# A linear-attention and routed-MLP block: how tile 3 is transposed, where the inverse deviation of the first tiles is computed, and two loads moved

## The chip, the cores and the metric

The kernel runs on one core of one Trainium2 chip. The metric is the device time of one launch in microseconds. The core's engines each run their own instruction queue in order: TensorE (PE, with its weight loads shown apart as PEld), VectorE (DVE), ScalarE (ACT), GpSimd (POOL) and SyncE (SP), which here only issues DMAs. Semaphores order them against each other.

## What is computed

x has 2048 rows (tokens) of 640 columns, in bf16. The result is the sum of three parts:

```python
xn  = layernorm(x)                       # (x - mean) / sqrt(var + 1e-5), per row
q, k, v = split(xn @ wqkv)               # 32 heads of 20 columns
phi(t) = where(t > 0, t + 1, exp(t)) + 1e-6
kv  = phi(k)^T v   per head              # sums over all 2048 rows
z   = sum over rows of phi(k)
A   = (phi(q) kv) / (phi(q) z) @ wo
r   = xn @ w_r;  the 8 rows with the largest r
y   = (silu(xn_sel @ w_gate) * (xn_sel @ w_up)) @ w_down * sigmoid(r_sel)
out = x + A + xn + (y added on the 8 chosen rows)
```

## The kernel before

The 2048 rows are 16 tiles of 128 rows; the 640 columns are 5 chunks of 128. The order of the instructions on every engine is the order in which the program writes them; the framework only adds the semaphore waits.

**Front part, tile by tile (t = 0 to 15).** For each tile:

- `ln_a`, `ln_b`, `ln_g` (VectorE): statistics of the left and the right half of the row, then mean and variance.
- `ln_r` (ScalarE): the inverse deviation `SR`, by a logarithm and an exponential.
- `ln_xn` (VectorE): the normalized tile, written to `XX[:, t, 0, :]`.
- The transposed tile `xnT`: tiles 0 to 3 by TensorE into PSUM (`tr_mm`, five 128x128 transposes in two halves) and from there by a copy on ScalarE or VectorE (`tr_cp`); tiles 4 to 15 by a DMA transpose issued on SP (`tr_dma`).
- `K` (TensorE): the tile's k, in two halves of 320 columns (the second half has one more, r), five matmuls each. For tiles 0 to 3 each half is cut again into chunks 0 and 1 (`KA`) and chunks 2 to 4 (`KB`), which are written between other work. The weights of the two halves, `wkh[0]` and `wkh[1]`, are loaded apart, the first on ScalarE's queue, the second on SP's.
- `PHe`, `PHr` (ScalarE) and `PHb` (VectorE): exponential, relu and their combination `pk`, that is phi(k).
- `G` (TensorE): sums of xn times phi(k) over the rows, accumulated in PSUM over all tiles, five matmuls of 512 columns and four of 128 for each tile. `ones(t)` (GpSimd) overwrites one column of the normalized tile with 1 after its transpose has been taken, so that `G` gives z too.

The first four tiles are written out by hand, interleaved; from tile 4 on a loop does `K(t)`, then `PHb(t-1)`, the normalization of tile t+2 with its DMA transpose, the phi of tile t, the statistics of tile t+3, and `G(t-1)`. Some turns of the loop also build constants on GpSimd (`pool_extra`).

**x on SP's queue.** Tiles 0 to 3 are loaded one by one, then the second half of the k weights, then tiles 4 to 7, 8 to 11 and 12 to 15 in three loads, then a DMA transpose of a block of zeros.

**After the front part.** The queries (`q_pe`, `q_fin`) follow in 20 steps, with the choice of the 8 rows, the gate and up products, the denominators and the folded output matrix between them, and at the end the output tiles. `bm2`, a mask made on GpSimd by `consts_e` and `bm2_copies`, is first used between the queries and the output.

The scratch tile for the phi of k and the PSUM banks matter for the order: `K` of tiles 0, 2 and 3 uses banks 6 and 7, that of tile 1 banks 4 and 5, the transposes of tiles 0 and 2 banks 0 and 1, those of tiles 1 and 3 banks 2 and 3, and `G` banks 0 to 5.

Of the kernel before, what the change touches and what calls it, by code (L numbers as in the profile page):

```python
# [7 lines left out]
P = 128  # L8
S = 2048
D = 640  # L10
# [3 lines left out]
T = S // P  # L14
KC = D // P
# [8 lines left out]
EPS_BF16 = 1.0013580322265625e-05  # L24
# [6 lines left out]
F32 = mybir.dt.float32  # L31
# [3 lines left out]
ALU = mybir.AluOpType  # L35
# [3 lines left out]
def kernel(  # L39
# [13 lines left out]
    pe, dve, act, pool, sp = nc.tensor, nc.vector, nc.scalar, nc.gpsimd, nc.sync  # L53

    x_v = A_x[0].rearrange("(t p) d -> p t d", p=P)
    out_v = out[0].rearrange("(t p) d -> p t d", p=P)
    wqkv_v = A_wqkv.rearrange("(kc p) n -> p kc n", p=P)
# [9 lines left out]
    def st(shape, dt, name, tag=None):  # L67
        return sb.tile(shape, dt, name=name, tag=tag or name)

    XX = st([P, T, 2, D], BF16, "XX")  # L70
# [10 lines left out]
    wu = st([P, KC, F], BF16, "wu")  # L81
# [5 lines left out]
    lowkey = st([P, T], I32, "lowkey")  # L87
    eps6 = st([P, 1], F32, "eps6")
    eps5 = st([P, 1], F32, "eps5")
    lnv = st([P, T], F32, "lnv")  # L90
    rbf = st([P, T], BF16, "rbf")
    MVf = st([P, T, 2], F32, "MVf")
    MV = MVf[:].bitcast(BF16).rearrange("p t (k o) -> p t k o", o=2)[:, :, :, 1]
    SR = st([P, T], F32, "SR")
# [3 lines left out]
    HW = 320  # L98
    wkh = [wk[:, :, 0:HW], wk[:, :, HW + 64 :]]


    def ld(eng, dst, src):
        eng.dma_start(dst, src)
# [7 lines left out]
    ld(act, wkh[0], wqkv_v[:, :, D : D + HW])  # L111
    ld(sp, XX[:, 1, 1, :], x_v[:, 1, :])
    ld(sp, XX[:, 2, 1, :], x_v[:, 2, :])
    ld(sp, XX[:, 3, 1, :], x_v[:, 3, :])
    ld(sp, wkh[1][:, :, 0:HW], wqkv_v[:, :, D + HW : 2 * D])
    for a, b in ((4, 8), (8, 12), (12, 16)):
        ld(sp, XX[:, a:b, 1, :], x_v[:, a:b, :])
    sp.dma_start_transpose(xnT[:, 0:4, S - P : S], zero[:])

    def warm4(w):  # L120
        pe.matmul(PS[:, 7, 0:w], lhsT=nc.const_aps.tensor(0.0, (P, P), F32),
                  rhs=nc.const_aps.tensor(0.0, (P, w), F32), start=True, stop=True)

    dve.memset(eps5[:], EPS_BF16)
    pool.memset(ident[:], 0.0)
    pool.affine_select(
        out=ident[:], in_=ident[:], compare_op=ALU.not_equal, fill=1.0,
# [19 lines left out]
    def ln_a(t):  # L147
        sts[t] = tmp.tile([P, 2, nc.vector.BN_STATS_DIM], F32, tag="stats", name="stats", bufs=4)
        dve.bn_stats(out=sts[t][:, 0, :], in_=XX[:, t, 1, 0:320])  # L149

    def ln_b(t):
        dve.bn_stats(out=sts[t][:, 1, :], in_=XX[:, t, 1, 320:D])  # L152

    def ln_g(t):
        dve.bn_aggr(out=MV[:, t, :], in_=sts[t][:])

    def ln_r(t):
        act.activation(lnv[:, t : t + 1], MV[:, t, 1:2], AF.Ln, bias=eps5[:])
        act.activation(SR[:, t : t + 1], lnv[:, t : t + 1], AF.Exp, scale=-0.5)  # L159

    def ln_xn(t, parts=((0, D),)):
        for a, b in parts:
            dve.tensor_scalar(out=XX[:, t, 0, a:b], in0=XX[:, t, 1, a:b], scalar1=MVf[:, t, 0:1],  # L163
                              scalar2=SR[:, t : t + 1], op0=ALU.subtract, op1=ALU.mult)
# [3 lines left out]
    def tr_mm(t, h, b0):  # L168
        k0, k1 = TRP[h]
        pt = PS[:, b0 + h, :].bitcast(BF16)  # L170
        for kc in range(k0, k1):
            pe.transpose(pt[:, (kc - k0) * P : (kc - k0 + 1) * P], XX[:, t, 0, kc * P : (kc + 1) * P], ident[:])  # L172

    def tr_cp(t, h, b0, eng):
        k0, k1 = TRP[h]
        src = PS[:, b0 + h, :].bitcast(BF16)[:, 0 : (k1 - k0) * P].rearrange("p (k c) -> p k c", c=P)
        dst = xnT[:, k0:k1, t * P : (t + 1) * P]
        if eng is act:
            act.copy(dst, src)  # L179
        else:  # L180
            dve.tensor_copy(dst, src)

    def tr_dma(t):
        sp.dma_start_transpose(xnT[:, :, t * P : (t + 1) * P], XX[:, t, 0, :])
# [14 lines left out]
    def off(t, h):  # L199
        return T - 1 - t if t != 1 and h else 0  # L200

    def K(t, hs=(0, 1), b=6, ks=range(KC)):
        for h in hs:
            if t > 4:
                pad(1)
            w = HW + h
            for kc in ks:
                pe.matmul(  # L208
                    PS[:, b + h, off(t, h) : off(t, h) + w],
                    lhsT=xnT[:, kc, t * P : (t + 1) * P],  # L210
                    rhs=wkh[h][:, kc, 0:w],
                    start=(kc == 0),
                    stop=(kc == KC - 1),
                )
# [3 lines left out]
    def phi_src(t, h, b):  # L218
        return PS[:, b + h, off(t, h) : off(t, h) + HW]

    def PHe(t, h, b=6):
        if t not in phis:
            phis[t] = tuple(tmp.tile([P, D], BF16, tag=k, name=k, bufs=3) for k in ("ek", "rk"))
        act.activation(phis[t][0][:, h * HW : (h + 1) * HW], phi_src(t, h, b), AF.Exp)  # L224

    def PHr(t, h, b=6):
        act.activation(phis[t][1][:, h * HW : (h + 1) * HW], phi_src(t, h, b), AF.Relu)  # L227
# [13 lines left out]
    def PHb(t):  # L241
        ek, rk = phis[t]
        dve.scalar_tensor_tensor(out=pk[:, t, :], in0=ek[:], scalar=1.0, in1=rk[:], op0=ALU.min, op1=ALU.add)  # L243

    def pad(n):
        for _ in range(n):
            pe.ldweights(zero[:, 0:P])  # L247

    def G(t, ks=range(KC)):
        for a in ks:  # L250
            lhsT = XX[:, t, 0, a * P : (a + 1) * P]
            pe.matmul(  # L252
                PS[:, a, :], lhsT=lhsT, rhs=pk[:, t, 0:512],
                start=(t == 0), stop=(t == T - 1),
            )
            if t > 4:
                pad(2)
            if a < 4:
                pe.matmul(  # L259
                    PS[:, 5, a * P : (a + 1) * P], lhsT=lhsT, rhs=pk[:, t, 512:D],  # L260
                    start=(t == 0 and a == 0), stop=(t == T - 1), skip_group_check=True,
                )

    def ones(t):
        pool.memset(XX[:, t, 0, ZD : ZD + 1], 1.0)  # L265
# [12 lines left out]
    def band(ap, base, n, w=DH):  # L278
        for k, (b0, sg) in enumerate(((base, 1), (w - 1 - base, -1))):
            pool.affine_select(  # L280
                out=ap, in_=ap, compare_op=ALU.is_ge, fill=0.0,
                base=b0, pattern=[[-sg * w, n], [0, w]], channel_multiplier=sg,
            )

    def consts_e():
        pool.memset(bm2[0:E2, :], 1.0)
        band(bm2[0:E2, :], P, 8)

    def bm2_copies(gs):
        for g in gs:  # L290
            pool.tensor_copy(bm2[32 * g : 32 * g + 32, :], bm2[0:E2, :])
# [14 lines left out]
    def consts_d():  # L306
        pool.iota(lowkey[:], pattern=[[P, T]], base=P - 1, channel_multiplier=-1)

    pool_extra = {3: consts_b, 4: consts_c, 5: consts_d}

    wo_v = A_wo.rearrange("(g r) d -> r g d", r=GC)
    wg_v = B_w_gate.rearrange("(kc p) n -> p kc n", p=P)
    wu_v = B_w_up.rearrange("(kc p) n -> p kc n", p=P)
# [18 lines left out]
                ld(sp, wg[:, k, :], wg_v[:, k, :])  # L332


    consts_e()
    bm2_copies((1, 2, 3))
    KA, KB = (range(0, 2), range(2, KC))
    ln_a(0)
    ln_b(0)
    ln_a(1)  # L340
    ln_g(0)
    ln_b(1)
    ln_r(0)
    ln_g(1)
    ln_xn(0, ((0, 2 * P),))
    ln_r(1)
    ln_xn(0, ((2 * P, D),))
    tr_mm(0, 0, 0)
    ln_xn(1)
# [5 lines left out]
    tr_cp(0, 1, 0, act)  # L355
    K(0, (0,), 6, KA)
    ln_b(2)
    tr_cp(1, 0, 2, act)
    tr_mm(1, 1, 2)
    ones(1)  # L360
    K(0, (0,), 6, KB)
    tr_cp(1, 1, 2, act)
    ln_g(2)
    ln_a(3)
    K(1, (0,), 4, KA)
    ln_r(2)
    ln_b(3)
    K(1, (0,), 4, KB)
    PHe(0, 0, 6)
    ln_xn(2)  # L370
    K(0, (1,), 6, KA)
    PHr(0, 0, 6)
    K(1, (1,), 4, KA)
    ln_g(3)
    ln_r(3)
    tr_mm(2, 0, 0)
    K(0, (1,), 6, KB)
    tr_cp(2, 0, 0, act)
    tr_mm(2, 1, 0)
    ones(2)  # L380
    ln_xn(3)
    K(1, (1,), 4, KB)
    PHe(0, 1, 6)
    tr_cp(2, 1, 0, dve)
    PHr(0, 1, 6)
    tr_mm(3, 0, 2)
    ln_a(4)
    K(2, (0,), 6, KA)
    rcopy1(5)
    PHe(1, 0, 4)  # L390
    tr_mm(3, 1, 2)
    ones(3)
    PHb(0)
    K(2, (1,), 6, KA)
    PHr(1, 0, 4)
# [4 lines left out]
    PHr(1, 1, 4)  # L400
    PHe(2, 0, 6)
    G(0, (4,))
    tr_cp(3, 0, 2, dve)
    ln_g(4)
    G(0, (0,))
    PHr(2, 0, 6)
    tr_cp(3, 1, 2, dve)
    G(0, (1,))
    ln_r(4)
    PHb(1)  # L410
    G(0, (2,))
    K(3, (0,), 6, KA)
    PHe(2, 1, 6)
    G(0, (3,))
    ln_xn(4)
    PHr(2, 1, 6)
    K(3, (0,), 6, KB)
    ln_a(5)
    tr_dma(4)
    ones(4)  # L420
    K(3, (1,), 6, KA)
    ln_b(5)
    PHe(3, 0, 6)
    G(1)
    PHr(3, 0, 6)
    ln_g(5)
    PHb(2)
    ln_r(5)
    ln_xn(5)
    K(3, (1,), 6, KB)  # L430
    tr_dma(5)
    ones(5)
    G(2)
    PHe(3, 1, 6)
    PHr(3, 1, 6)
    ln_a(6)
    ln_b(6)
    ln_g(6)
# [53 lines left out]
    for t in range(T - 1):  # L492
# [13 lines left out]
                      op0=ALU.arith_shift_right, op1=ALU.bitwise_and)  # L506
# [21 lines left out]
    def z_ev():  # L528
        dve.tensor_copy(zs[:, 0:512], PS[0:1, 4, :])
        dve.tensor_copy(zs[:, 512:D], PS[0:1, 6, 0:P])  # L530
        ld(sp, zcol[:], zs[:])
# [275 lines left out]
    q_fin(0, 0)  # L807
    q_pe(0, 1, 7)
    z_ev()
    for k0, k1 in ((0, 3), (3, KC)):  # L810
        ld(sp, wu[:, k0:k1, :], wu_v[:, k0:k1, :])
    q_pe(0, 2, 1)
    q_fin(0, 1)
    q_pe(0, 3, 2)
# [137 lines left out]
```

## Time and profile before

| | |
|---|---|
| median of 3 runs | 105.94 us (105.9 to 106.11) |
| the profiled execution | 105.91 us |
| its span (first to last instruction) | 104.2 us |
| TensorE busy | 99.8 us (96% of the span) |
| VectorE busy | 82.7 us (79%) |
| ScalarE busy | 69.1 us (66%) |
| GpSimd busy | 17.1 us (16%) |
| TensorE's granted clock | full in all 40 slices |
| bytes moved by DMA | 19.77 MB, 190 GB/s on average |

Times in the profile are microseconds from the start of the span. A row of a timeline has start, duration, engine, line of the kernel, operation, what it writes and reads with the shape, how many are merged in the row, and in brackets how long the engine was idle before it and what ended the wait. A row of a group has, after the bar, the busy time and the mean duration in ns. A row of DMA issues has the bytes of one and the microseconds from issue to landing. "PE" with line 208 is `K`, 172 `tr_mm`, 252 and 259 `G`; "DVE" with line 149, 152 and 155 is `ln_a`, `ln_b` and `ln_g`, 163 `ln_xn`, 181 `tr_cp`, 243 `PHb`; "ACT" with 158 and 159 is `ln_r`.

### The profile page before, as it was taken

To read this page: it belongs to the slowest core of one execution; us is meant where nothing else is said; L and a number is where in the kernel's file an instruction comes from. 1 tells how busy PE (TensorE), PEld (TensorE's weight loads), DVE (VectorE), ACT (ScalarE), POOL (GpSimd) and SP (SyncE) were. 2 spreads that over 40 slices of the span, in tenths; PEclk is the share of its full clock that TensorE was granted. 3 is DMA by queue.
4 is the path that set the end of the run, shared out by engine and by line. 5 is a ranking of instruction groups with operands and counts; after the bars stand their busy time and mean duration, and the time that the engine had idled before them with its cause. 6 is when DMAs were issued, how large, how long until landed. Compare 5 with 4: busy or idle time off the path is not lost.

```text
span 104.2 us, 2816 instructions
## 1 busy us (share of the span) xinstructions
PE 99.8 (96%) x944; PEld 72.5 (70%) x1176; DVE 82.7 (79%) x186; ACT 69.1 (66%) x174; POOL 17.1 (16%) x57
## 2 busy tenths in 40 slices
PE   6999999999999999999999999999999999999980
PEld 3347666668888888888877777875577667777760
DVE  1797999988888898873887886778988997888870
ACT  4289957666666666888599989997983997000000
POOL 7700000620000000000000064460001500000500
PEclk9999999999999999999999999999999999999999
DMA  2999937334557755889999999901760039983344
GB/s 63 298 307 377 325 66 69 66 66 92 135 127 92 140 124 124 191 248 359 224 399 249 360 406 382 319 22 31 217 236 9 12 110 270 280 289 122 126 129 126
DMA packets 23408, 19.77 MB, mean 190 GB/s; under 512 B 10978, under 2 KB 21858, under 8 KB 23394
## 3 DMA queue, kind: packets, MB, share of 16 engines
q1 hardware_dynamic: 22152, 19.11, 63.2%
q10 hardware_dynamic: 954, 0.46, 1.7%
q8 instruction: 8, 0.13, 0.6%
q0 software_dynamic: 288, 0.01, 0.3%
q14 instruction: 6, 0.05, 0.2%
HBM read 13.80 MB, written 3.65 MB: 168 GB/s over the span
## 4 chain that ended last, share of the span: by engine, by line
PE 89%; DVE 3%; DMA 2%; issue 2%; DVEq 0%
PE PS L208 21%; PE PS L480 21%; PE PS L751 20%; PE PS L252 16%; PE PS L259 4%; DMA XX<-in_A_x_dram 2%; PE PS L708 2%; PE PS L672 1%; PE PS L551 1%; PE PS L172 1%; PE PS L727 1%; PE PS L273 1%; DVE stats L149 1%; DVE XX L163 1%; DVE stats L152 1%
## 5 line engine op out<-in xcount | busy, mean ns | idle before, releaser
L208 PE MATMUL PS<-wk,xnT 128*128 128x320 bf16 (+1 forms) x160 | 25.2, 300 | 0.0
L252 PE MATMUL PS<-pk,XX 128*128 128x512 bf16 x75 | 22.7, 379 | 0.0
L247 PEld LDWEIGHTS <-zero 128*128 128x128 bf16 x224 | 18.2, 97 | 5.7
L480 PE MATMUL PS<-xnT,wq 128*128 128x512 bf16 x97 | 21.8, 379 | 0.3 <-issue 0.2
L751 PE MATMUL PS<-Mb,pqT 128*128 128x320 bf16 (+4 forms) x165 | 22.1, 295 | 0.0
L224 ACT ACTIVATE ek<-PS 128x320 bf16<-128x320 f32 x32 | 14.1, 441 | 9.9 <-PE PS L208 9.9
L751 PEld LDWEIGHTS <-pqT 128*128 128x128 bf16 x165 | 15.8, 98 | 4.5 <-issue 0.2
L208 PEld LDWEIGHTS <-xnT 128*128 128x128 bf16 x160 | 15.1, 97 | 4.5 <-ACT xnT L179 0.2
L243 DVE SCALAR_TENSOR_TENSOR pk<-ek,rk 128x640 bf16<-128x640 bf16 x16 | 13.1, 820 | 4.8 <-ACT rk L227 4.5
L542 DVE SCALAR_TENSOR_TENSOR pqT<-qe,qr 128x512 bf16<-128x512 bf16 x20 | 13.5, 682 | 2.5 <-ACT qr L489 2.5
L488 ACT ACTIVATE qe<-PS 128x512 bf16<-128x512 f32 x20 | 12.5, 624 | 2.9 <-PE PS L480 2.3
L259 PE MATMUL PS<-pk,XX 128*128 128x128 bf16 x64 | 14.0, 219 | 0.3
L227 ACT ACTIVATE rk<-PS 128x320 bf16<-128x320 f32 x32 | 14.0, 437 | 0.0
L480 PEld LDWEIGHTS <-wq 128*128 128x128 bf16 x100 | 11.6, 118 | 2.9
L489 ACT ACTIVATE qr<-PS 128x512 bf16<-128x512 f32 x20 | 12.5, 626 | 0.0
L760 DVE TENSOR_TENSOR o<-PS,XX 128x640 bf16<-128x640 f32 x11 | 9.0, 823 | 2.9 <-PE PS L751 1.4
L252 PEld LDWEIGHTS <-XX 128*128 128x128 bf16 x80 | 7.8, 98 | 4.5
L196 ACT ACTIVATE XX<-XX,MR,SR 128x640 bf16<-128x640 bf16 x11 | 9.4, 913 | 0.0
L149 DVE BATCH_NORM_STATS2 stats<-XX 128x6 f32<-128x320 bf16 x16 | 7.4, 461 | 2.0 <-DMA XX<-in_A_x_dram 2.0
L163 DVE TENSOR_SCALAR XX<-XX,MVf,SR 128x640 bf16<-128x640 bf16 (+2 forms) x17 | 7.2, 433 | 0.6 <-ACT SR L159 0.6
L152 DVE BATCH_NORM_STATS2 stats<-XX 128x6 f32<-128x320 bf16 x16 | 7.7, 482 | 0.0
L265 POOL MEMSET XX<- 128x1 bf16 x18 | 1.9, 107 | 35.4 <-DVE XX L163 15.5
(111 smaller groups left out, 102.1 us busy)
## 6 DMA issues: line engine op xcount, KB each, us to landing
out_dram<-o SPq DMA_DIRECT2D x15, 160.0 KB, 2.7
XX<-in_A_x_dram SPq DMA_DIRECT2D x3, 640.0 KB, 7.9
wg<-in_B_w_gate_dram SPq DMA_DIRECT2D x5, 384.0 KB, 7.7
wd<-in_B_w_down_dram SPq DMA_DIRECT2D x1, 1920.0 KB, 13.3
wu<-in_B_w_up_dram SPq DMA_DIRECT2D x1, 1152.0 KB, 6.3
wv<-in_A_wqkv_dram SPq DMA_DIRECT2D x5, 160.0 KB, 2.6
wq<-in_A_wqkv_dram SPq DMA_DIRECT2D x1, 800.0 KB
hi_d<-XX SPq DMA_DIRECT2D x1, 800.0 KB, 4.0
```

What stands on the lines that cost most here:

```text
L208: pe.matmul(PS[:, b + h, off(t, h) : off(t, h) + w], lhsT=xnT[:, kc, t * P : (t + 1) * P], rhs=wkh[h][:, kc, 0:w], start=(kc == 0), stop=( ...
L224: act.activation(phis[t][0][:, h * HW : (h + 1) * HW], phi_src(t, h, b), AF.Exp)
L227: act.activation(phis[t][1][:, h * HW : (h + 1) * HW], phi_src(t, h, b), AF.Relu)
L243: dve.scalar_tensor_tensor(out=pk[:, t, :], in0=ek[:], scalar=1.0, in1=rk[:], op0=ALU.min, op1=ALU.add)
L247: pe.ldweights(zero[:, 0:P])
L252: pe.matmul(PS[:, a, :], lhsT=lhsT, rhs=pk[:, t, 0:512], start=(t == 0), stop=(t == T - 1),)
L259: pe.matmul(PS[:, 5, a * P : (a + 1) * P], lhsT=lhsT, rhs=pk[:, t, 512:D], start=(t == 0 and a == 0), stop=(t == T - 1), skip_group_check= ...
L480: pe.matmul(PS[:, bank, :], lhsT=by5(wq[:, kc, :])[:, m, :], rhs=xnT[:, kc, tb * TBLK : (tb + 1) * TBLK], start=(kc == 0), stop=(kc == KC ...
L488: act.activation(e, PS[:, bank, :], AF.Exp)
L489: act.activation(r, PS[:, bank, :], AF.Relu)
L542: dve.scalar_tensor_tensor(out=pqT[:, m, tb * TBLK : (tb + 1) * TBLK], in0=e, scalar=1.0, in1=r, op0=ALU.min, op1=ALU.add,)
L751: pe.matmul(PS[:, b, o : o + c1 - c0], lhsT=pqT[:, kc, t * P : (t + 1) * P], rhs=Mb[:, kc, c0:c1], start=(kc == 0), stop=(kc == KC - 1))
```

## The change

- Tile 3 is transposed by a DMA on SP instead of five transposes on TensorE and two copies on VectorE. Its `K` is no longer spread over the sums of tiles 0 and 1 but stands behind `G(1)`, in whole halves; `PHe(3, ...)`, `PHr(3, ...)` and the instructions around it move with it.
- The inverse deviation of tiles 0 to 3 is computed on GpSimd, by an add of the epsilon and a power of -0.5 (`ln_p`), instead of two instructions on ScalarE. A constant column of -0.5 is set by VectorE at the start.
- On VectorE the first part of `ln_xn(0)` stands ahead of `ln_g(1)`; `ln_a(3)` and `ln_b(3)` stand behind `ln_xn(2)`.
- On SP the second half of the k weights is loaded ahead of x of tile 3. The load of x of tiles 12 to 15 moves behind the DMA transpose of tile 3.
- The mask `bm2` is made in the loop's turn for tile 7 instead of at the start; the two loads of the up weights become one.

```diff
+    mhalf = st([P, 1], F32, "mhalf")
...
     ld(sp, XX[:, 1, 1, :], x_v[:, 1, :])
     ld(sp, XX[:, 2, 1, :], x_v[:, 2, :])
+    ld(sp, wkh[1][:, :, 0:HW], wqkv_v[:, :, D + HW : 2 * D])
     ld(sp, XX[:, 3, 1, :], x_v[:, 3, :])
-    ld(sp, wkh[1][:, :, 0:HW], wqkv_v[:, :, D + HW : 2 * D])
-    for a, b in ((4, 8), (8, 12), (12, 16)):
+    for a, b in ((4, 8), (8, 12)):
         ld(sp, XX[:, a:b, 1, :], x_v[:, a:b, :])
     sp.dma_start_transpose(xnT[:, 0:4, S - P : S], zero[:])
...
+    dve.memset(mhalf[:], -0.5)
...
+    def ln_p(t):
+        pool.tensor_scalar(out=lnv[:, t : t + 1], in0=MV[:, t, 1:2], scalar1=EPS_BF16, scalar2=None, op0=ALU.add)
+        pool.tensor_tensor(out=SR[:, t : t + 1], in0=lnv[:, t : t + 1], in1=mhalf[:], op=ALU.pow)
...
+    def consts_f():
+        consts_e()
+        bm2_copies((1, 2, 3))
-    pool_extra = {3: consts_b, 4: consts_c, 5: consts_d}
+    pool_extra = {3: consts_b, 4: consts_c, 5: consts_d, 6: consts_f}
...
-    consts_e()
-    bm2_copies((1, 2, 3))
     KA, KB = (range(0, 2), range(2, KC))
     ln_a(0)
     ln_b(0)
     ln_a(1)
     ln_g(0)
+    ln_p(0)
     ln_b(1)
-    ln_r(0)
+    ln_xn(0, ((0, 2 * P),))
     ln_g(1)
-    ln_xn(0, ((0, 2 * P),))
-    ln_r(1)
+    ln_p(1)
     ln_xn(0, ((2 * P, D),))
     tr_mm(0, 0, 0)
     ln_xn(1)
...
     ln_b(2)
+    ln_g(2)
+    ln_p(2)
...
     tr_cp(1, 1, 2, act)
-    ln_g(2)
-    ln_a(3)
     K(1, (0,), 4, KA)
-    ln_r(2)
-    ln_b(3)
     K(1, (0,), 4, KB)
     PHe(0, 0, 6)
     ln_xn(2)
+    ln_a(3)
+    ln_b(3)
     K(0, (1,), 6, KA)
     PHr(0, 0, 6)
     K(1, (1,), 4, KA)
     ln_g(3)
-    ln_r(3)
+    ln_p(3)
     tr_mm(2, 0, 0)
     K(0, (1,), 6, KB)
     tr_cp(2, 0, 0, act)
     tr_mm(2, 1, 0)
     ones(2)
     ln_xn(3)
+    tr_dma(3)
+    ones(3)
+    ld(sp, XX[:, 12:T, 1, :], x_v[:, 12:T, :])
     K(1, (1,), 4, KB)
     PHe(0, 1, 6)
     tr_cp(2, 1, 0, dve)
     PHr(0, 1, 6)
-    tr_mm(3, 0, 2)
     ln_a(4)
...
-    tr_mm(3, 1, 2)
-    ones(3)
     PHb(0)
...
     G(0, (4,))
-    tr_cp(3, 0, 2, dve)
     ln_g(4)
     G(0, (0,))
     PHr(2, 0, 6)
-    tr_cp(3, 1, 2, dve)
     G(0, (1,))
     ln_r(4)
     PHb(1)
     G(0, (2,))
-    K(3, (0,), 6, KA)
     PHe(2, 1, 6)
     G(0, (3,))
     ln_xn(4)
     PHr(2, 1, 6)
-    K(3, (0,), 6, KB)
     ln_a(5)
     tr_dma(4)
     ones(4)
-    K(3, (1,), 6, KA)
+    G(1)
     ln_b(5)
-    PHe(3, 0, 6)
-    G(1)
-    PHr(3, 0, 6)
     ln_g(5)
+    K(3, (0,), 6)
     PHb(2)
     ln_r(5)
+    PHe(3, 0, 6)
     ln_xn(5)
-    K(3, (1,), 6, KB)
+    K(3, (1,), 6)
+    PHr(3, 0, 6)
     tr_dma(5)
     ones(5)
-    G(2)
     PHe(3, 1, 6)
     PHr(3, 1, 6)
+    G(2)
...
-    for k0, k1 in ((0, 3), (3, KC)):
-        ld(sp, wu[:, k0:k1, :], wu_v[:, k0:k1, :])
+    ld(sp, wu[:], wu_v)
```

## The prediction

> **What bounds the kernel now.** The page first: how long the span is, which engine is full, and what the chain of waits is made of.
>
> ```profile
> span 104.2 us, 2816 instructions
> PE   6999999999999999999999999999999999999980
> PE 89%; DVE 3%; DMA 2%; issue 2%; DVEq 0%
> ```
>
> TensorE is full in every slice but the first and the last, and 89% of the chain is its own instructions. So the time is a start, then a block of matmuls without a gap, then a short end. Only two things can move it: matmul work taken out of the block, and a gap put in front of it or into it. The profiled execution took 105.91 us, 1.71 more than its span; the median of the runs is 105.94, so the sum below is made against 105.91 and carries over as it is.
>
> The chain in order of time shows where the block begins, and where the change touches it.
>
> ```profile
> 5.54 0.80 DVE XX L163 x2
> 6.38 0.29 PE PS L172 x2
> ...
> 9.90 0.13 PE PS L172 x2
> 10.03 0.27 PE PS L208 x2
> 10.30 0.17 PE PS L172 x3
> 10.47 1.09 PE PS L208 x8
> 11.56 0.22 PE PS L252
> ```
>
> Up to 6.3 us the normalization of tiles 0 and 1 on VectorE is the chain; from 6.38, the first transposes of tile 1, it is TensorE alone. The five L172 pieces at 9.90 and 10.30 are the transposes of tile 3. At 11.56 the sums G(0) begin (the record of their first matmul starts at 11.40, since a record begins before the array streams). Next, the engine that feeds this stretch: VectorE's timeline (start, duration).
>
> ```profile
> 4.48 0.20 DVE L155 BATCH_NORM_AGGREGATE MVf<-stats 128x2 bf16<-128x12 f32 x1
> ...
> 5.27 1.05 DVE L163 TENSOR_SCALAR XX<-XX,MVf,SR 128x256 bf16<-128x256 bf16 x3
> 6.23 0.49 DVE L149 BATCH_NORM_STATS2 stats<-XX 128x6 f32<-128x320 bf16 x1
> 6.64 0.48 DVE L152 BATCH_NORM_STATS2 stats<-XX 128x6 f32<-128x320 bf16 x1
> 7.15 0.21 DVE L155 BATCH_NORM_AGGREGATE MVf<-stats 128x2 bf16<-128x12 f32 x1
> 7.27 0.44 DVE L149 BATCH_NORM_STATS2 stats<-XX 128x6 f32<-128x320 bf16 x1
> 7.63 0.48 DVE L152 BATCH_NORM_STATS2 stats<-XX 128x6 f32<-128x320 bf16 x1
> 8.08 0.45 DVE L163 TENSOR_SCALAR XX<-XX,MVf,SR 128x640 bf16<-128x640 bf16 x1
> 8.44 0.20 DVE L155 BATCH_NORM_AGGREGATE MVf<-stats 128x2 bf16<-128x12 f32 x1
> 9.24 0.45 DVE L163 TENSOR_SCALAR XX<-XX,MVf,SR 128x640 bf16<-128x640 bf16 x1 [0.60 <-ACT SR L159]
> 9.61 0.35 DVE L181 COPY xnT<-PS 128x384 bf16<-128x384 bf16 x1
> 9.87 0.49 DVE L149 BATCH_NORM_STATS2 stats<-XX 128x6 f32<-128x320 bf16 x1
> 10.27 0.81 DVE L243 SCALAR_TENSOR_TENSOR pk<-ek,rk 128x640 bf16<-128x640 bf16 x1
> ...
> 19.03 0.83 DVE L243 SCALAR_TENSOR_TENSOR pk<-ek,rk 128x640 bf16<-128x640 bf16 x1
> 19.77 0.44 DVE L163 TENSOR_SCALAR XX<-XX,MVf,SR 128x640 bf16<-128x640 bf16 x1
> ```
>
> The three L163 of the 5.27 row end at 6.32; the last, ln_xn(1), is one of 0.45, so it began at 5.87. The row at 10.27 is PHb(0), which ends at 11.08; G(0) reads its pk. (The two rows at 19 us serve a question below.) So G(0) had 0.32 us to spare, and a VectorE that comes to PHb(0) later than that stops TensorE. This is the place that decides.
>
> **The price of the moved deviation.** Now it is two ScalarE instructions, of which the first stands here, with the first matmul of G(0).
>
> ```profile
> 4.71 0.29 ACT L158 ACTIVATE lnv<-MVf,eps 128x1 f32<-128x1 bf16 x1 [0.63 <-DVE MVf L155]
> 11.40 0.38 PE L252 MATMUL PS<-pk,XX 128*128 128x512 bf16 x1
> ```
>
> From the end of the aggregate (4.68) to the L163 that uses the result (5.27) are 0.59 us, with a hop of 0.03 at its start (4.68 to 4.71), and I take the same at its end. The new path is hop, add on GpSimd, its wait for its own result, power, hop; call it p. No row shows a power on GpSimd. The nearest:
>
> ```profile
> L265 POOL MEMSET XX<- 128x1 bf16 x18 | 1.9, 107 | 35.4 <-DVE XX L163 15.5 <-DMA xnT<-XX 12.9 <-DVE MVf L155 3.2
> L291 POOL COPY bm<-bm 32x160 bf16<-32x160 bf16 x3 | 0.9, 310 | 0.1
> L651 POOL COPY kv<-kv 32x40 bf16<-32x40 bf16 x4 | 0.8, 210 | 1.3 <-DVE kv L640 1.2
> 18.88 0.12 POOL L295 MEMSET bm<- 128x32 f32 x1
> 19.08 0.85 POOL L297 TENSOR_SCALAR_AFFINE_SELECT bm<-bm 128x32 f32<-128x32 f32 x1
> L297 POOL TENSOR_SCALAR_AFFINE_SELECT bm<-bm x2: 288/568/849, 19.1 to 20.0; 128x32 f32<-128x32 f32 x2
> ```
>
> The copies give 0.10 us for 120 columns more, so one column costs 0.18; the memset at 18.88 ends at 19.00 and the select that needs it starts at 19.08, a wait of 0.08. I take 0.18 for the add and, for want of a nearer row, as much for the power: p = 0.03 + 0.18 + 0.08 + 0.18 + 0.03 = 0.50. Lower end: both as cheap as a memset, 0.10, p = 0.34. Upper end: the add like the quicker of the selects of L297 (0.29), the power like their mean (0.57), p = 1.00. The path itself is thus worth about what ScalarE's is; what counts is how often VectorE now stands and waits for it.
>
> **The change step by step, at p = 0.50.**
>
> Tile 0 and 1: ln_xn(0)'s first part now comes before ln_g(1). Power of tile 0 at 4.68 + 0.50 = 5.18; first part to ln_g(1) 0.27 (5.27 to the 5.54 of the chain), ln_g(1) 0.21 (as at 7.15), end 5.66. Its power ends at 6.16, where ln_xn(1) starts, 0.29 later than now. ln_xn(0)'s rest (0.36) lies inside that wait. The two deviations, side by side before, are in series now.
>
> Tile 2: ln_a(2) follows 0.36 on, ln_b(2) 0.41, ln_g(2) 0.51, its end 0.21 (rows from 5.87 to 7.36: 1.49). Before, ln_a(3) and ln_b(3) filled the wait for the deviation; the change moves them behind ln_xn(2), so VectorE idles for p: ln_xn(2) at 6.16 + 1.49 + 0.50 = 8.15, against 8.08.
>
> Tile 3: ln_a(3) 0.36 later, at 8.51, then the same 0.41, 0.51 and 0.21 to the end of ln_g(3) at 9.64, and p again: ln_xn(3) at 10.14, against 9.24. That is 0.90 later.
>
> From there the order is unchanged: copy of tile 2, ln_a(4), PHb(0), which ends 1.84 after ln_xn(3) starts (9.24 to 11.08): 11.98. TensorE's first matmul starts some 0.08 behind it (ln_xn(1) ends at 6.32, its transposes stand at 6.38), at 12.06. Before it was 11.40. Hence **+0.66 us**.
>
> What TensorE saves in front of that: the five transposes, 0.13 + 0.17 = 0.30. Without a stall G(0) would come 0.30 earlier; with it the 0.30 only lengthens the stall, so I count it at nothing. It would count in full if PHb(0) ended by 11.0.
>
> The second weight half and x of tile 3 swap on SP's queue.
>
> ```profile
> 2.68 0.43 SPq L103 DMA_DIRECT2D wk<-in_A_wqkv_dram  x1
> wk<-in_A_wqkv_dram SPq DMA_DIRECT2D x1, 400.0 KB, 5.4
> xnT<-XX SPq DMA_TRANSPOSE x12, 3.2
> xnT<-zero SPq DMA_TRANSPOSE x1, 8.0
> ```
>
> The later of the two lands at 2.68 + 5.4 = 8.1 now, with the same bytes ahead of it after the swap; so x of tile 3 lands near 8.1, under the 8.51 at which ln_a(3) wants it: nothing at p = 0.50. At p = 0.34 ln_a(3) could go at 8.03 and waits for it, 0.1.
>
> Tile 3's transpose by DMA: issued at the end of ln_xn(3), 10.6, landing 3.2 later, 13.8. K(3) is behind G(0) and G(1), ten matmuls of 0.22 after 12.06 at the least, so not before 14.2: covered by 0.4. The zero transpose took 8.0 because it stood behind all x loads; the load of tiles 12 to 15 (640 KB) no longer stands in front. That load waits on SP behind tile 3's transpose, and tile 4's transpose behind both; its cover is K(3) and G(2). x of tile 12 is first read in turn 8 of the loop. ones(3) waits for the transpose on GpSimd, with only other ones behind it, and the last power is ahead. Two copies of tile 3 leave VectorE behind PHb(0), 0.6 us that G(1)'s PHb(1) can use: no gap of its own between G(0) and G(1). ScalarE loses eight small instructions; it is not what PHb(0) waits for then. The mask constants moved to turn 7 (about 2 us of GpSimd, used only after the queries) and the joined load of wu (one issue less on SP, weights wanted late) are counted at nothing; cover: GpSimd's idle time of 2.5 us a turn, and the whole query stage.
>
> Sum: 105.91 + 0.66 = 106.57, said as 106.6. In p it is four waits in a row (ln_xn(3) at 8.14 + 4p), so 0.1 more in p is 0.4 in the time. The ends: p = 0.34 with x at 8.1 gives ln_xn(3) at 9.6, G(0) at 11.5, 106.0; p = 1.00 gives ln_xn(3) 12.14, G(0) 14.06, 108.6.
>
> **A rule weighed.** The row first: the two selects of L297 are the same instruction, one took 0.85 us, the other 0.29; the first began at 19.08 with the pass of 19.03 to 19.86 running, the second at 20.0 with the L163 of 19.77 to 20.21. The Trainium skill, GPSIMD Engine Reference, section 8 (Key points), says that GpSimd shares its SBUF interfaces with VectorE and contends with VectorE instructions in a two-port mode or with two SBUF inputs; by that the first select was held, and the trace agrees; the second, beside a one-input pass, does not show it. By that rule the sum would be 106.8, without it 106.6; the working is the first rival.
>
> **Rivals.**
> *GpSimd is held by VectorE.* Tile 1's add comes at 5.69, while ln_xn(0)'s rest (0.36, from about 5.57) still runs; if it is held until 5.93, ln_xn(1) and all behind it are 0.24 later: 106.8. For it: the 0.85 of L297. Against: the 0.29 of the second. Part of the slower cases, 0.12. The page of the Trainium skill named above speaks for this one.
> *The transposes' gain comes through: faster.* G(0) stands the whole 0.30 earlier if ln_xn(3) starts by 9.16, which needs p = 0.26 (8.14 + 4p) and x of tile 3 by 7.8: 105.6. It turns faster at all below ln_xn(3) = 9.48, p = 0.33. For it: the durations on GpSimd are rough, and its waits may overlap; one of ScalarE's deviations now takes 0.72 (aggregate end 7.36 to 8.08), since ScalarE is crowded. Against: both of GpSimd's instructions would have to be cheaper than a memset, and x of tile 3 now arrives last. 0.13.
> *It cancels.* p of 0.33 to 0.38, G(0) within 0.2 of 11.40: 105.9 to 106.1. 0.14.
> *Late transposes or a slow power.* If tile 3's or 4's transpose lands like the zero one did, or the power costs a microsecond, TensorE stops again: tile 3 landing at 10.6 + 8.0 = 18.6, where K(3) is due at 14.2 or later, would cost up to 4.4 more, 111; a power of 1 us, p = 1.3, gives ln_xn(3) at 13.3 and 109.8. Against: the queue has 640 KB less in front. 0.07.
>
> **How the numbers follow.** The forecast (VectorE reaches PHb(0) late, +0.2 to +1.6) has 0.54, its held form 0.12, together with the last rival 0.73 for slower by over 0.2%, about what a measurement of this kernel can tell from no change (0.21 us); same 0.14, faster 0.13. The range leaves out 0.1 on either side: from 105.75, into the faster case, to 107.5, a p of 0.73. The slower case alone lies in 106.1 to 107.6.
>
> **What would show it.** In the changed profile: VectorE idle ahead of the L163 of tiles 0, 1, 2 and 3, ended by GpSimd, each near 0.5; L163 of tile 3 at about 10.1; PHb(0) ending near 12.0; TensorE idle ahead of the first L252, ended by VectorE, and no gap behind it; no L172 of tile 3. The prediction is wrong if GpSimd's two instructions together take under 0.25, if TensorE's first L252 starts before 11.4, or if K(3) or K(4) shows a wait for a DMA.

## The result and the profile after

| | before | after |
|---|---|---|
| median of 5 runs each | 105.94 us (105.85 to 106.12) | 108.55 us (108.47 to 108.59) |
| profiled execution (its span) | 105.91 us (104.2) | 108.48 us (106.8) |
| first matmul of G(0), its record | 11.40 | 14.06 |
| from there to the last piece of the chain of waits (101.43 and 104.01) | 90.0 | 90.0 |

The ratio is 1.0241, 95% interval 1.0227 to 1.0255: slower by 2.6 us, where +0.66 was forecast. The last row of the table (101.43 − 11.40 and 104.01 − 14.06) says where: everything lies ahead of G(0), nothing behind it. Some executions of one kernel take longer than its others, by up to 3.7 us among the experiments below, and no run here shows why; so positions in the profiles are read beside the medians.

VectorE's timeline after, from the first normalization to PHb(0). In the changed kernel's lines `ln_a`, `ln_b`, `ln_g` are 151, 154, 157, `ln_xn` is 169, `tr_cp` 187, `PHb` 249; GpSimd's add and power are 164 and 165.

```profile
5.58 0.35 DVE L169 TENSOR_SCALAR XX<-XX,MVf,SR 128x256 bf16<-128x256 bf16 x1 [0.66 <-POOL SR L165]
5.84 0.20 DVE L157 BATCH_NORM_AGGREGATE MVf<-stats 128x2 bf16<-128x12 f32 x1
5.96 0.33 DVE L169 TENSOR_SCALAR XX<-XX,MVf,SR 128x384 bf16<-128x384 bf16 x1
7.06 0.45 DVE L169 TENSOR_SCALAR XX<-XX,MVf,SR 128x640 bf16<-128x640 bf16 x1 [0.77 <-POOL XX L271]
7.43 0.48 DVE L151 BATCH_NORM_STATS2 stats<-XX 128x6 f32<-128x320 bf16 x1
7.83 0.47 DVE L154 BATCH_NORM_STATS2 stats<-XX 128x6 f32<-128x320 bf16 x1
8.34 0.21 DVE L157 BATCH_NORM_AGGREGATE MVf<-stats 128x2 bf16<-128x12 f32 x1
9.55 0.45 DVE L169 TENSOR_SCALAR XX<-XX,MVf,SR 128x640 bf16<-128x640 bf16 x1 [1.00 <-POOL SR L165]
9.91 0.49 DVE L151 BATCH_NORM_STATS2 stats<-XX 128x6 f32<-128x320 bf16 x1
10.31 0.47 DVE L154 BATCH_NORM_STATS2 stats<-XX 128x6 f32<-128x320 bf16 x1
10.82 0.21 DVE L157 BATCH_NORM_AGGREGATE MVf<-stats 128x2 bf16<-128x12 f32 x1
12.04 0.45 DVE L169 TENSOR_SCALAR XX<-XX,MVf,SR 128x640 bf16<-128x640 bf16 x1 [1.00 <-POOL SR L165]
...
13.07 0.81 DVE L249 SCALAR_TENSOR_TENSOR pk<-ek,rk 128x640 bf16<-128x640 bf16 x1
```

VectorE stands in front of each tile's normalization, 0.66, 0.77, 1.00 and 1.00 us, each time for GpSimd (the row that names L271, a memset, is the same wait: the memset is a short instruction right behind the power). Tile 3 is normalized at 12.04 instead of 9.24, and PHb(0) ends at 13.88 instead of 11.08. G(0), which reads its result, begins behind it:

```profile
14.06 0.38 PE L258 MATMUL PS<-pk,XX 128*128 128x512 bf16 x1
```

GpSimd's timeline has what VectorE waits for (tiles 0, 1 and 2; tile 3 is like tile 2):

```profile
4.65 0.24 POOL L164 TENSOR_SCALAR lnv<-MVf 128x1 f32<-128x1 bf16 x1 [1.80 <-DVE MVf L157]
4.97 0.57 POOL L165 TENSOR_TENSOR SR<-lnv,mhalf 128x1 f32<-128x1 f32 x1
6.14 0.23 POOL L164 TENSOR_SCALAR lnv<-MVf 128x1 f32<-128x1 bf16 x1 [0.59 <-DVE MVf L157]
6.46 0.57 POOL L165 TENSOR_TENSOR SR<-lnv,mhalf 128x1 f32<-128x1 f32 x1
...
8.64 0.22 POOL L164 TENSOR_SCALAR lnv<-MVf 128x1 f32<-128x1 bf16 x1 [1.56 <-DVE MVf L157]
8.95 0.57 POOL L165 TENSOR_TENSOR SR<-lnv,mhalf 128x1 f32<-128x1 f32 x1
```

The power of one column takes 0.57 us. For tile 2 the whole path, from the end of the aggregate (8.55) to the normalization (9.55), is a hop of 0.09, the add 0.22, a wait of 0.09, the power 0.57 and a hop of 0.03: 1.00 us.

The chain of waits tells it differently, and has to be read with care. From 7.57 on it names TensorE alone:

```profile
7.06 0.46 DVE XX L169
7.57 0.29 PE PS L178 x2
...
8.51 3.09 PE PS L214 x12
```

The twelve L214, matmuls of the k of tiles 0 and 1, took 1.70 before and take 3.09 now. The table by stretch shows why (length, then busy time of PE, PEld, DVE, ACT, POOL, then the granted clock, the share of the DMA engines and GB/s):

```profile
4.52:7.93 3.41, 1.73 (x11) 0.61 (x10) 1.97 (x8) 0.89 (x3) 1.67 (x5) 1.00 1.01 320
7.93:11.34 3.41, 3.41 (x17) 2.08 (x15) 2.04 (x6) 1.58 (x4) 1.06 (x4) 0.50 1.09 316
```

TensorE, busy for only 1.73 of 3.41 us while it waited for the first two tiles, got half the clock for the next 3.41 us. So two explanations stand: G(0) waits for VectorE, held by GpSimd; or G(0) waits for k matmuls that ran at half speed.

### The profile page after: what moved, and what is told of

It is laid out like the page before. It is cut to its first block, busy times and chain, and to the rows that moved or that the text cites. A ratio compares the mean times of both kernels' runs of the same rounds, so it can differ in the third digit from the quotient of the medians.

```text
span 106.8 us, 2807 instructions
## 1 busy us (share of the span) xinstructions
PE 100.8 (94%) x939; PEld 73.3 (69%) x1171; DVE 82.4 (77%) x185; ACT 67.8 (63%) x166; POOL 20.9 (20%) x65
## 4 chain that ended last, share of the span: by engine, by line
PE 88%; DVE 3%; DMA 2%; issue 2%; POOL 2%; DVEq 0%; POOLq 0%
PE PS L214 22%; PE PS L484 20%; PE PS L755 19%; PE PS L258 15%; PE PS L265 4%; DMA XX<-in_A_x_dram 2%; PE PS L712 2%; PE PS L676 1%; POOL SR L165 1%; PE PS L555 1%; PE PS L731 1%; PE PS L279 1%; DVE stats L151 1%; PE PS L178 1%; DVE XX L169 1%
## 5 line engine op out<-in xcount | busy, mean ns | idle before, releaser
L214 PE MATMUL PS<-wk,xnT 128*128 128x320 bf16 (+1 forms) x160 | 26.2, 312 | 0.0
L214 PEld LDWEIGHTS <-xnT 128*128 128x128 bf16 x160 | 16.0, 102 | 5.3 <-issue 0.2
L271 POOL MEMSET XX<- 128x1 bf16 x18 | 2.0, 114 | 28.7 <-DMA xnT<-XX 15.1
```

The costliest lines, as they stand in the source:

```text
L214: pe.matmul(PS[:, b + h, off(t, h) : off(t, h) + w], lhsT=xnT[:, kc, t * P : (t + 1) * P], rhs=wkh[h][:, kc, 0:w], start=(kc == 0), stop=( ...
```

## Experiments

Theory: VectorE's chain sets G(0); the price of the deviation on GpSimd (1.00 us) enters four times, because the new order of the statistics leaves VectorE nothing to do in the meantime. Rivals: the order of the statistics alone; the halved clock; something in the DMA transposes. The kernel before ran beside each group of experiments: 105.92 us median (17 runs) with the first four kernels, 106.03 (11 runs) with the second four, 106.00 (23 runs) with the last four.

**The deviation back on ScalarE, everything else as in the change.**

```diff
-    ln_p(t)      # t = 0, 1, 2, 3
+    ln_r(t)
```

> The changed kernel with the inverse deviation of tiles 0 to 3 back on ScalarE; order, loads and the DMA transpose stay as changed. Theory S (VectorE waits for the deviation four times in a row, so the time goes by four times its latency p): p falls from about 1.0 us to 0.59 us where ScalarE is free, the normalization of tile 3 starts at 8.0 + 4 x 0.59 = 10.4 us instead of 12.04, the sums of tile 0 follow near 12.4 instead of 14.06: 106.9 us, up to 107.1 if ScalarE is late once. Rival L (the swapped loads or the DMA transpose cost the time): 108.3 or more. Rival C (TensorE's halved clock behind the idle stretch costs it): 107.2 or less, but then with the halved clock gone while VectorE still comes late.

107.44 us median (107.05 to 108.09, 4 runs), ratio 1.0161 (1.0126 to 1.0196); the profiled execution 107.14. That is a little above the expected 106.9 to 107.1; the expected positions (10.4 and 12.4) came out at 10.41 and, for G(0), 12.57. VectorE's normalizations of tiles 1 to 3:

```profile
6.24 0.45 DVE L169 TENSOR_SCALAR XX<-XX,MVf,SR 128x640 bf16<-128x640 bf16 x1 [0.36 <-ACT SR L161]
...
8.32 0.45 DVE L169 TENSOR_SCALAR XX<-XX,MVf,SR 128x640 bf16<-128x640 bf16 x1 [0.60 <-ACT SR L161]
...
10.41 0.45 DVE L169 TENSOR_SCALAR XX<-XX,MVf,SR 128x640 bf16<-128x640 bf16 x1 [0.60 <-ACT SR L161]
```

Tile 3 is normalized 1.63 us earlier than in the change, but still 1.17 later than before: with a cheaper deviation the new order alone keeps VectorE waiting four times.

**The power on the variance itself** (the kernel leaves out the epsilon, so each deviation is one GpSimd instruction).

```diff
-        pool.tensor_scalar(out=lnv[:, t : t + 1], in0=MV[:, t, 1:2], scalar1=EPS_BF16, scalar2=None, op0=ALU.add)
-        pool.tensor_tensor(out=SR[:, t : t + 1], in0=lnv[:, t : t + 1], in1=mhalf[:], op=ALU.pow)
+        pool.tensor_tensor(out=SR[:, t : t + 1], in0=MV[:, t, 1:2], in1=mhalf[:], op=ALU.pow)
```

> The changed kernel without the add of the epsilon: the power is taken of the variance itself, so the epsilon is left out of the result. One of GpSimd's two instructions is gone, 0.24 us and the gap of 0.07 behind it. Theory S, four in a row: 108.5 - 4 x 0.31 = 107.25 us. If only the tiles 2 and 3 count: 107.9. If the latency counts once: 108.2. Rival C: if the halved clock is what holds and it stays, 107.7 or more.

Its four runs scatter (107.14, 107.79, 108.89, 109.03; ratio 1.0250, 1.0207 to 1.0293), so the expected time was met by one of them only, the profiled one, and the median settles nothing; the positions in the profile do. Its normalizations of the four tiles (`ln_xn` is line 168 here):

```profile
5.27 0.34 DVE L168 TENSOR_SCALAR XX<-XX,MVf,SR 128x256 bf16<-128x256 bf16 x1 [0.34 <-POOL SR L164]
...
6.43 0.45 DVE L168 TENSOR_SCALAR XX<-XX,MVf,SR 128x640 bf16<-128x640 bf16 x1 [0.45 <-POOL SR L164]
...
8.58 0.45 DVE L168 TENSOR_SCALAR XX<-XX,MVf,SR 128x640 bf16<-128x640 bf16 x1 [0.67 <-POOL XX L270]
...
10.73 0.45 DVE L168 TENSOR_SCALAR XX<-XX,MVf,SR 128x640 bf16<-128x640 bf16 x1 [0.66 <-POOL XX L270]
```

They start 0.31, 0.63, 0.97 and 1.31 us earlier than in the change: one step more at each tile. One add with the wait behind it is 0.22 + 0.09 = 0.31. The time of this profiled execution is 1.34 lower than the change's. So the price does enter four times.

**TensorE kept busy** by two matmuls of 256 columns that nobody reads.

```diff
+    warm4(256)
     tr_mm(0, 0, 0)
...
     tr_mm(0, 1, 0)
+    warm4(256)
```

> The changed kernel with two more throwaway matmuls of 256 columns, one ahead of the first transpose of tile 0 and one behind its last, so that TensorE is not idle there. Theory S: the granted clock stays full, the matmuls of tiles 0 and 1 end earlier, and the time does not move (108.3 to 108.6 us), because VectorE still reaches the first phi at 13.9. Rival C: the twelve matmuls that took 3.1 us take 1.7, and the time falls by about as much, to 107.2.

108.54, 108.64, 109.72 and 110.28 us (ratio 1.0308, 1.0264 to 1.0353), so certainly no gain, and two runs well above the expected 108.3 to 108.6; the profiled one is 108.54, and its clock is full throughout:

```profile
4.52:7.93 3.41, 2.95 (x15) 1.35 (x14) 1.98 (x8) 0.85 (x2) 1.66 (x5) 1.00 1.07 362
7.93:11.34 3.41, 3.35 (x29) 2.19 (x28) 2.08 (x7) 2.43 (x7) 1.01 (x4) 1.00 1.04 293
```

G(0)'s first record is at 14.06, as in the change. TensorE now has idle time in front of it, and the chain of waits names what was hidden:

```profile
9.60 0.45 DVE XX L169
10.04 0.40 DVE stats L151
10.44 0.40 DVE stats L154
...
10.87 0.22 DVE MVf L157
11.09 0.08 issue
11.17 0.23 POOL lnv L164
11.40 0.07 issue
11.48 0.57 POOL SR L165
...
13.19 0.73 DVE pk L249
13.93 0.14 issue
14.06 0.59 PE PS L258 x2
```

This is the loop: normalization, two statistics, aggregate, add, power, and the next normalization; at its end PHb(0) (line 249) lets G(0) go. The rival falls: the half clock only filled time in which TensorE would have waited. One of the change's own five runs had the clock at full, too, and took 108.47.

**Old order with GpSimd, and with ScalarE.** Two kernels that differ in nothing but the place of the four deviations; both have tile 3's DMA transpose, the later mask and the joined load of the change, and the statistics and early loads in the order of before.

```diff
 # transpose_only                     # old_order
     ln_r(t)                          ln_p(t)
```

> The kernel before with the transposed-tile part of the change alone: tile 3 by DMA, its k behind the sums of tile 1, x of tiles 12 to 15 loaded behind that transpose, the mask late, one load of the up weights; deviation on ScalarE, statistics in the order of before, x of tile 3 ahead of the second weight half. Theory: five transposes (0.30 us) leave TensorE; the sums of tile 0 can start 0.08 behind the first phi, which ends at 11.08 as before: 11.16 instead of 11.40, that is 105.7 us. Rival L: the transpose of tile 3 or 4 lands late and TensorE waits in front of their k: 106.2 or more.

> The changed kernel with the four inverse deviations on GpSimd, but the statistics and the two early loads in the order of the kernel before; it differs from transpose_only only in where the four deviations are worked out. Theory (the price of the power and the new order each cost, and the order made four prices stand in series): with the add 0.23, the power 0.57, two hops and a wait, about 1.0 us from the mean and variance to the normalization. Here other statistics stand between: ln_xn(0) at 5.6, ln_xn(1) near 6.5 (behind ln_xn(0)), ln_xn(2) near 9.0, ln_xn(3) near 10.6, first G(0) near 12.5 against 11.38 in transpose_only; time 106.9 to 107.3. Rival (the order does not matter, only the price): four prices as in the changed kernel, ln_xn(3) near 12, time near 108.5. Second rival (the price is nothing, the order is all): ln_xn(3) near 9.2, time near 106.0.

transpose_only: 106.03 us median (12 runs), ratio 1.0008 (0.9988 to 1.0028), so the DMA transpose and what came with it cost nothing that these runs can tell, and gain nothing either; 105.7 was expected. old_order: 106.96 us median (106.89 to 108.75, 4 runs), ratio 1.0084 (1.0054 to 1.0114), as expected; its normalizations of tiles 1 to 3:

```profile
6.45 0.45 DVE L169 TENSOR_SCALAR XX<-XX,MVf,SR 128x640 bf16<-128x640 bf16 x1 [0.23 <-POOL SR L165]
...
8.94 0.45 DVE L169 TENSOR_SCALAR XX<-XX,MVf,SR 128x640 bf16<-128x640 bf16 x1 [0.25 <-POOL SR L165]
...
10.50 0.45 DVE L169 TENSOR_SCALAR XX<-XX,MVf,SR 128x640 bf16<-128x640 bf16 x1 [1.00 <-POOL XX L271]
```

With the statistics of tile 3 between the aggregate and the normalization of tile 2, the wait there is 0.25 instead of 1.00. Together with the two kernels above this gives a square (median; in brackets the profiled execution and its first record of G(0)). Beside the order of the statistics, the two early loads differ between its columns.

| deviation on | order of before | order of the change |
|---|---|---|
| ScalarE | 106.03 (106.24; 11.22) | 107.44 (107.14; 12.57) |
| GpSimd | 106.96 (106.93; 12.48) | 108.55 (108.48; 14.06) |

At G(0), where the change acts, GpSimd costs 1.26 us in the old order and 1.49 in the new; the new order costs 1.35 with ScalarE and 1.58 with GpSimd. By the medians the same four are 0.9, 1.1, 1.4 and 1.6, with scalar_dev's runs spread over 1 us; by the profiled executions 0.7, 1.3, 0.9 and 1.55. The two that rest on transpose_only's profiled time are low because that execution takes 95.0 us beyond its G(0), where the other three take 94.4 to 94.6. Neither alone makes the 2.6: both count, and at G(0) each is 0.23 dearer with the other, as the theory has it, since the order decides at how many tiles the price is met without cover.

**The move to GpSimd alone, in the kernel before.** `ln_r` becomes `ln_p` for tiles 0 to 3, the mask is made later as in the change, TensorE transposes tile 3.

> The kernel before with only the four inverse deviations moved to GpSimd (and the mask constants later, as the change has them), tile 3 transposed by TensorE as before. Theory: as in old_order the price shows at ln_xn(0) (+0.35), then at tiles 2 and 3, ln_xn(3) near 10.6 against 9.24, G(0) near 12.7 against 11.56; time 106.9 to 107.3. Rival (TensorE's transposes of tile 3 then fill the wait, and something later hides it): under 106.4.

107.16 us median (106.92 to 108.05, 4 runs), ratio 1.0123 (1.0081 to 1.0166): as expected. Tile 3 is normalized at 10.64.

**Where the transposes' gain went.** transpose_only takes five transposes off TensorE. The chain from tile 2's k to the first sum, in that kernel:

```profile
9.43 0.68 PE PS L214 x5
10.11 0.02 issue
10.13 1.25 PE PS L214 x8
11.38 0.43 PE PS L258 x2
```

From 9.43 to 11.38 are 1.95 us. Before, the same k with the transposes took 2.07 (9.49 to 11.56). So 0.12 of the 0.30 is left; the last eight k matmuls, 1.09 before, take 1.25. The traces show what takes back the 0.16. The first of the eight belongs to the second half of tile 2's k and writes bank 7, which still holds the second half of tile 0's k until its relu (`PHr`, line 233 on ScalarE) has read it. That relu ends at 10.08 and the eight begin at 10.13, on a TensorE that has run empty at 10.11. In row_one_later, a kernel with the same front part (below), the chain of waits names it:

```profile
10.24 0.34 ACT rk L233
10.58 0.04 issue
10.62 1.25 PE PS L214 x8
```

Before, the transposes of tile 3 stood between the relu's end (10.14) and these matmuls (10.31). That is read from the traces; no run takes the wait away. Later in this execution VectorE waits longer for the row of routing scores:

```profile
58.05 1.22 DVE L600 MAX8 k<-krow 1x8 f32<-1x1024 f32 x1 [0.64 <-DMA krow<-c]
```

Before, the same wait was 0.21. The row's DMA is issued at 52.1, among the five loads of the gate weights (45 to 53 us on SP), and lands 6.0 us later. Two ways to clear it were tried, by moving those loads, and a third by moving VectorE's maximum; each with a control that does the same to the kernel before.

```diff
 # wg_late: removed from loads(13), added behind z_ev(); gate_early: one at each of tiles 8 to 12
-            for k in range(KC):
-                ld(sp, wg[:, k, :], wg_v[:, k, :])
...
+        if 8 <= t < 8 + KC:
+            ld(sp, wg[:, t - 8, :], wg_v[:, t - 8, :])
 # row_one_later
-    route2()
     q_fin(0, 4)
     q_pe(1, 1, 2)
+    route2()
```

> transpose_only, with the five loads of the gate weights (1.92 MB) issued after the sum's column instead of at 45 to 53 us, so that the routing row does not land behind them. Theory (the transposes' 0.18 us was given back at the routing row, which landed 6.0 us after its issue): the row lands in about 3 us, VectorE does not wait for it at 57 to 58 us, and the 0.16 to 0.3 us come through: 105.5 to 105.75 against 106.0 of transpose_only and 105.9 of before; and if before loses its own 0.21 there too, the control wg_late_before gets 105.7. Rival (the gate weights then arrive late for their matmuls at 67.5): those matmuls wait, 106.3 or more. Rival (the row's landing is not what sets the time): 106.0 as transpose_only.

> The kernel before with only the five loads of the gate weights issued after the sum's column. Control for wg_late_best. Theory: VectorE's wait of 0.21 us for the routing row goes, 105.7; wg_late_best should then be 0.1 to 0.2 below this one, which is the worth of the transposes with the cover of the row taken away. Rival (no wait there set the time): 105.9, no change.

108.20 us (ratio 1.0188, 1.0160 to 1.0215) and 107.78 us (1.0167, 1.0134 to 1.0200), both far from what was expected. VectorE's wait for the row is gone in both (in the first it lands in 1.9 us), but the up weights, pushed back, are late:

```profile
69.85 1.00 PE L710 MATMUL PS<-wu,xsT 128*32 128x384 bf16 x20 [1.36 <-DMA wu<-in_B_w_up_dram]
```

In the control the same wait is only 0.34, and TensorE's longest is 1.23 us, for a product that VectorE makes ahead of the output's matmuls (at 79.08); what delays it stays open.

> transpose_only, with the five loads of the gate weights issued one each at tiles 8 to 12 (about 27 to 40 us) instead of together at 45 to 53 us; the weights of the up projection then start earlier too. Theory (the routing row is what took the transposes' gain): the row lands in about 2 us as in wg_late_best, VectorE's 0.64 us in front of the maximum of the row goes, and nothing arrives late this time: 105.4 to 105.75, against 106.0 of transpose_only. Rival (the extra 1.92 MB among the transposes by DMA delays one of them, and a K waits): over 106.2. Rival (what followed the row's wait absorbs it again, ScalarE's queue or the denominators): 105.9 to 106.1.

> The kernel before with only the gate weights' loads one each at tiles 8 to 12. Control for gate_early. Theory: VectorE's 0.21 us for the routing row goes, 105.65 to 105.85; gate_early stays 0.1 to 0.3 below it, which is then the worth of tile 3's transpose by DMA. Rival (the wait set nothing): 105.9 to 106.0.

107.35 us (106.49 to 110.15; ratio 1.0104, 1.0069 to 1.0140) and 108.20 us (107.42 to 109.14; 1.0188, 1.0148 to 1.0228): again not as expected. With the 1.92 MB among them, transposes by DMA come late, and k waits for two of them (in the control too, 0.79 and 1.09); the longer wait:

```profile
47.87 1.52 PE L214 MATMUL PS<-wk,xnT 128*128 128x320 bf16 x10 [1.16 <-DMA xnT<-XX]
```

> transpose_only, with VectorE's maximum of the routing row and its five small instructions put one block of the queries later in VectorE's order (behind the fifth block's sum); no load is moved. Theory: the row has landed when VectorE comes to it, ScalarE's wait of 1.00 us for a query buffer shrinks to about 0.4, and the time is 105.4 to 105.8. Rival (the gathered rows then come late for the gate matmuls at 67.8): 106.0 or more, with TensorE waiting ahead of them.

> The kernel before with only the maximum of the routing row one block later. Control for row_one_later. Theory: it loses 0.21 us of VectorE's wait, 105.7 to 105.9; row_one_later stays 0.1 to 0.3 below it. Rival: no change, 105.9 to 106.0.

105.87 us (105.56 to 106.54, 12 runs; ratio 0.9989, 0.9969 to 1.0008) and 105.93 us (105.73 to 106.34, 12 runs; ratio 0.9990, 0.9970 to 1.0009). VectorE comes to the row without a wait in both, but both are just above what was expected (105.4 to 105.8 and 105.7 to 105.9), neither is told apart from the kernel before, nor the two from each other. So the transpose of tile 3 by DMA is worth at most about 0.1 to 0.2 us here, and whether it is worth anything stays open.

## Why the prediction was wrong in size

**The step that failed** is the price of the deviation, "for want of a nearer row, as much for the power": 0.18 us, where the power takes 0.57. The other terms of p were close: the add 0.22 to 0.24 for 0.18, the wait 0.07 to 0.09 for 0.08, the hop to GpSimd 0.08 to 0.10 for 0.03, the hop back 0.03. p was 1.00 instead of 0.50, and the power makes 0.39 of the difference. In the forecast's own form, four waits in a row, that is 4 x 0.50 = 2.0 us on 106.57, or 108.6; the profiled execution took 108.48.

**The form held.** ln_xn(3) at 8.14 + 4p gives 12.14 for p = 1.00 (measured 12.04), for the 0.60 that VectorE waits in scalar_dev 10.54 (10.41), and for the 0.66 in no_eps_add 10.78 (10.73). PHb(0) ends 1.84 after ln_xn(3) starts in the change, as assumed. The upper end worked out ahead, p = 1.00 with G(0) at 14.06 and 108.6, is what came, within 0.1 us. That it agrees to the hundredth is luck: the mean of two selects of 0.29 and 0.85 says nothing of a power, and at G(0) two small errors cancel, an aggregate of tile 0 that starts 0.11 earlier than in the profile before and a first matmul 0.18 behind PHb(0) instead of 0.08. The range was cut off at p = 0.73 all the same, with that mean of 0.57 us already quoted. The choice went to the copy because it had the same shape; the shape said nothing about an operation of another kind, and the term had a factor of four.

**The list of what would show it.** Right: VectorE idle ahead of each of the four normalizations, ended by GpSimd; no L172 of tile 3; no wait of a K for a DMA. Wrong in size: each idle time (0.66 to 1.00 for 0.5), tile 3 at 12.04 for 10.1, PHb(0)'s end at 13.88 for 12.0. Not seen as described: TensorE idle ahead of G(0), since the halved clock stretched the k matmuls over it. None of the three signs of being wrong came: two of them guarded against a change that is cheaper than forecast, the third against late transposes, and none against a dearer power.

**The rivals.** GpSimd held by VectorE: no. The add that this rival names, of tile 1, starts at 6.14 in the change while the rest of ln_xn(0) runs (5.96 to 6.29), and takes 0.23 like the others; in old_order the power of tile 1 starts at 5.84 while a normalization runs (5.58 to 6.22), and takes 0.57 like the others. Both passes have one tensor as input. A select of the mask beside PHb, with two, took 0.85 again in the change. The transposes' gain comes through: no, not even alone (106.03). Late transposes: none in the change. The slow power, put into the last rival at p = 1.3 and 0.07 together with late transposes, was the right mechanism.

**The swapped loads** show no cost: ln_a(3) follows ln_xn(2) without a wait in the change (9.91) and in scalar_dev, and no k waits for its weights there. No run moves them alone.

## What to carry to other kernels

A term that no row shows and that enters the sum several times deserves a range as wide as its nearest rows of any kind, times its count; the likeliest value must not be the row of the same shape but another operation. Before moving a short computation to an idle engine, ask what the consumer does meanwhile: here the statistics of the next tile hid much of its latency, and taking them out of that gap cost about as much as the slower engine. When the chain of waits names an engine that runs at half clock, ask whether it only fills time it would have waited.

## What the runs showed of the hardware

A power of one column of 128 values on GpSimd takes 0.57 us, an add of the same shape 0.22 to 0.24, and the hop from VectorE 0.08 to 0.10 where the hop to ScalarE is 0.03.

TensorE's clock was halved for one stretch of 3.41 us after a stretch of the same length in which it was busy 1.73 us; with 2.95 us of work there (kept_busy) it was not, and in one of the change's own five runs the mean clock was full as well. The Trainium skill, TensorE: Matmul & The Clock Gate, Part 1, gives a free-running window of 3413 ns and half the clock after an idle one; the trace agrees on the length, while the stretch ahead of the halved one was half busy here and not idle. Where that earlier window begins no trace shows, so how busy is busy enough stays open.
